# Attention with two gated layers on one core: paired softmax sums, a later second frame, and a regrouped last chunk

## The chip, the cores and the metric

The kernel runs on one core of a Trainium2 chip. The metric is the device time in microseconds of one execution, as the median of several runs. The profile of one execution gives what each engine did and when.

## What is computed

The reference has three parts, on batch 4, sequence 576 and 8 heads of 64. The first is causal attention with a decay that comes from a running sum along the sequence:

```python
cum = np.cumsum(np.maximum(s, 0.0), axis=-1)
scores = scale * q @ k.T + np.minimum(-(cum[..., :, None] - cum[..., None, :]), 0.0)
attn = exp(scores - max);  attn = attn / (attn.sum(-1) + 1e-9);  out = attn @ v
```

The second is a layer of width 1024 with a three-tap convolution and a gate: `h = relu(x @ w_in)`, `(h * sigmoid(conv(h))) @ w_out`. The third mixes along the sequence at rank 32, `u = x + (x.T @ U @ V).T`, and returns `u + relu(u @ w_ch1) @ w_ch2` with 2048 hidden channels.

## The kernel before

All 32 heads run one after the other (`att_head`). A head's scores are made in five blocks of query rows: `scores` takes blocks 0 to 3 of 128 rows, and `scores4` the last 64 rows of two heads at once, in two halves of 288 keys. For each block TensorE multiplies (L690), VectorE adds the mask and finds the row's extreme (L651), ScalarE takes the exponential and the row sum (L668), VectorE adds 1e-9 to the sum and inverts it (L724 and L725 for the four sums of blocks 0 to 3, L763 and L769 for the last block), and GpSimd multiplies the block by the inverse (L679, in `normalise`). TensorE then transposes the block (`transp`, L793) and multiplies it with v (`av`, L829).

Beside this the weights are brought from memory as 64-bit numbers, decoded by ScalarE (L502) and VectorE (L505 once, L515 twice for each piece), and split into a high and a low part (L353 on ScalarE, L365 on GpSimd). The first layer of a batch (`m1_in`, `m1_out`) runs while the attention of the next one does. Then come the sequence mixing (`mix`), the first product of the third part as a seven-product Strassen scheme (`m2_in`, L1178, with sums `S` of weight blocks at L1140 and `T` of activations at L1077), and its second product.

That second product runs in five chunks of tokens, four of 512 and a last one of 256. Of each chunk, `m2_load` brings hidden block f (16 of them), and `m2_out` adds three products for each of four output blocks dt (L1277, 128 rows each) into four accumulators `my`. When f is 15, each accumulator is scaled and added to `u` on VectorE (L1300) and stored (L1308). The hidden blocks sit in a ring of five pairs of tiles, `mh` and `ml`, so block 15 is loaded into the tiles that block 10 leaves.

What sets the order of all of this is a planner. Every step is an entry of a list with an engine, a modelled cost and its dependencies; `Plan.order` simulates the engines with those costs and takes on each engine the ready entry that stands first in the list. The instructions are then issued in that order, and each engine works its own row through in order. So a changed cost, or a dependency that is added, moves instructions of other steps too.

At the start, two tiles `qkFs`, one each for the first two heads, get a frame: VectorE clears 64 rows (L451), and ScalarE's queue brings two rows of ones (L454). The running sum `cum` is brought (L447), clipped (L459) and summed (L460); rows of it go into the tiles (L579 on SP's queue, L582 on ScalarE's). q and k come by L577, v by L591, the mask by L1317, and a unit matrix `ident` by L1323, with two shifted halves of it by L1328.

Transfers of the SP and ScalarE queues share eight completion semaphores (DMAHW0 to DMAHW7), which are handed out in turn. A transfer whose semaphore was used before waits, at the head of its queue, until that earlier transfer has landed.

Of the kernel before, what the change touches and what calls it, by code (L numbers as in the profile page):

```python
# [24 lines left out]
NF1, NF2 = 8, 16  # L25
# [8 lines left out]
NG = 4  # L34
WN = ("A11", "A12", "A22", "S1", "S2", "S3", "S4")
UN = ("B11", "B21", "B22", "T1", "T2", "T3", "T4")

WI, WO, WP, WM = 0.3, 1.5, 0.3, 0.2

# [270 lines left out]
def tile_attention_moe_mixer(  # L310
# [133 lines left out]
    def cum():  # L444
        return cc()

    dma(73728, lambda: nc.sync.dma_start(out=cum(), in_=s), [], [cc])  # L447
    key = [cc]
    for t in qkFs:

        dve(2 * S, lambda t=t: nc.vector.memset(t[0:64], 0.0), [], [(t, "z"), (t, "r0"), (t, "r1")], True)  # L451
        for i in range(2):
            dma_act(
                lambda t=t, i=i: nc.scalar.dma_start(out=t[i : i + 1, i, :], in_=one_d[i, 0:1, 0, :]),  # L454
                [],
                [(t, "z")],
            )

    dve(S, lambda: nc.vector.tensor_scalar(cum(), cum(), 0.0, 8.0, ALU.max, ALU.mult), key, key, True)  # L459
    scan = dve(S, lambda: nc.vector.tensor_tensor_scan(cum(), cum(), cum(), 0.0, ALU.add, ALU.max), key, key)  # L460

    def decay_parts():
        hi_dve(lambda: rk[:, 0, :], cum, key, [(rk, 0)], S)
# [236 lines left out]
    def scores(h, i):  # L700
        P, sm = st[h]["P"][i], st[h]["sm"]
        w = 128 * i + 128
        ps = bank("sc", f"sc{h}_{i}")
        products(h, ps, 128, 128 * i, 0, w)
        top(ps, 128, w, 384 - 128 * i, lambda: sm[:, i : i + 1], None, [], (sm, f"m{i}"))
        exps(
            lambda: P[:, :w],
            ps,
            128,
            w,  # L710
            lambda: sm[:, i : i + 1],
            lambda: sm[:, 4 + i : 5 + i],
            (sm, f"m{i}"),
            [P, (sm, f"s{i}")],
        )
        if i in RECIP:
            ns = range(max((x + 1 for x in RECIP if x < i), default=0), i + 1)
            ss = [(sm, f"s{n}") for n in ns]
            rs = [(sm, f"r{n}") for n in ns]

            def r():
                return sm[:, 8 + ns[0] : 9 + i]

            dve(2, lambda: nc.vector.tensor_scalar(r(), sm[:, 4 + ns[0] : 5 + i], 1e-9, None, ALU.add), ss, rs)  # L724
            dve(15, lambda: nc.vector.reciprocal(r(), r()), rs, rs)  # L725
            for n in ns:
                Pn = st[h]["P"][n]
                normalise(Pn, 128 * n + 128, lambda n=n: sm[:, 8 + n : 9 + n], (sm, f"r{n}"), [Pn])

    def scores4(h):  # L730

        P, sm = st[h]["P"][4], sm4s[h // 2 % 2]
        tiles = []
        for n in range(2):
            ps = bank("sc", f"sc{h}_4_{n}")

            products(h + 1, ps, 128, S - 128, n * HS, HS)
            products(h, ps, 64, S - 64, n * HS, HS)
            top(
                ps,  # L740
                128,
                HS,
                512 * n,
                lambda n=n: sm[:, n : n + 1],
                None if n == 0 else lambda: sm[:, 0:1],
                [] if n == 0 else [(sm, "m0")],
                (sm, f"m{n}"),
            )
            tiles.append(ps)
        for n, ps in enumerate(tiles):  # L750
            exps(
                lambda n=n: P[:, n * HS : n * HS + HS],
                ps,
                128,
                HS,
                lambda: sm[:, 1:2],
                lambda n=n: sm[:, 2 + n : 3 + n],
                (sm, "m1"),
                [(P, n), (sm, f"s{n}")],
            )  # L760
        dve(
            60,
            lambda: nc.vector.scalar_tensor_tensor(  # L763
                sm[:, 4:5], sm[:, 2:3], 1e-9, sm[:, 3:4], ALU.add, ALU.add
            ),
            [(sm, "s0"), (sm, "s1")],
            [(sm, "r")],
        )
        dve(15, lambda: nc.vector.reciprocal(sm[:, 4:5], sm[:, 4:5]), [(sm, "r")], [(sm, "r")])  # L769
        normalise(P, S, lambda: sm[:, 4:5], (sm, "r"), [(P, 0), (P, 1)])  # L770


# [490 lines left out]
        )  # L1263
        hid[c, f] = (mh, ml)

    def m2_out(c, f):
        n, t0 = CHUNKS[c], offs[c]
        mh, ml = hid.pop((c, f))
        if f == 0:
            ys[c] = [bank("my", f"my{c}_{dt}") for dt in range(KT)]  # L1270
        for dt in range(KT):

            def mms(dt=dt):
                c0 = dt * 128
                wh, wl = w2h[f][:, c0 : c0 + 128], w2l[f][:, c0 : c0 + 128]
                for k, (ww, xx) in enumerate(((wh, mh), (wh, ml), (wl, mh))):
                    nc.tensor.matmul(  # L1277
                        ys[c][dt][:, :n], lhsT=ww, rhs=xx[:, :n], start=f + k == 0, stop=f == NF2 - 1 and k == 2
                    )

            pe(3 * mm(n), mms, [w2h[f], w2l[f], mh, ml], [ys[c][dt]])
        if f == NF2 - 1:
            for dt in range(KT):
                o = ring(m2, "o", RINGS["o"], [128, 512], F32, f"o{c}_{dt}")
                t = t0
                while t < t0 + n:
                    b = t // S
                    e = min(t0 + n, (b + 1) * S)
                    dma(
                        (e - t) * 512,  # L1290
                        lambda o=o, t=t, e=e, b=b, dt=dt: nc.sync.dma_start(
                            out=o[:, t - t0 : e - t0], in_=u_t[b][:, dt, t - b * S : e - b * S]
                        ),
                        [(u_d[b], dt)],
                        [(o, t)],
                    )
                    t = e
                dve(
                    n,
                    lambda o=o, dt=dt: nc.vector.scalar_tensor_tensor(  # L1300
                        o[:, :n], ys[c][dt][:, :n], 2.0**-16, o[:, :n], ALU.mult, ALU.add
                    ),
                    [ys[c][dt], o],
                    [o],
                )
                dma(
                    n * 512,
                    lambda o=o, dt=dt: nc.sync.dma_start(out=outT[dt, :, t0 : t0 + n], in_=o[:, :n]),  # L1308
                    [o],
                    [],  # L1310
                )


    prep4(0)
# [10 lines left out]
    for a in (0, 64):  # L1325
# [2 lines left out]
            lambda a=a: nc.sync.dma_start(out=ident[:, 128 + a : 192 + a], in_=ident_d[:, 64 - a : 128 - a]),  # L1328
            [],
            [(ident, 1 + a)],  # L1330
        )

    w1_jobs = [(f, c) for c in (0, 512) for f in range(NF1)]

# [167 lines left out]
    for g in range(2):  # L1502
        blk = (w2a, u1p)[g].buf(f"u{g}", [128, 2 * 7 * S], F32R, f"w2_{g}")
        for i in range(7):
            f = 7 * g + i
            w2h[f] = Part(blk, lambda t, i=i: t[:, 1024 * i : 1024 * i + 512], f"w2h_{f}")
            w2l[f] = Part(blk, lambda t, i=i: t[:, 1024 * i + 512 : 1024 * i + 1024], f"w2l_{f}")

    def load_w2b(f):
        load_split(w2[f], w2h[f], w2l[f], 512, 512, f"w2b_{f}")  # L1510
# [16 lines left out]
    for n in range(len(seq) + LAG):  # L1527
# [3 lines left out]
                n2 += 1  # L1531
            m2_load(*seq[n])
        if n >= LAG:
            m2_out(*seq[n - LAG])
    for p in (m2, mx, u1p, w2a, dec, banks):
        end = p.close()
        end.preds.update(o for o in plan.ops[:-1] if o.eng == "-")
# [57 lines left out]
```

## Time and profile before

| | |
|---|---|
| median of 3 runs | 851.01 us (849.09 to 852.35) |
| the profiled execution | 849.4 us, of which 847.6 us from the first instruction to the last |
| TensorE busy | 813.4 us, 96% of the span |
| VectorE, ScalarE, GpSimd busy | 606.6, 471.0, 392.7 us |
| granted TensorE clock | 0.999 of full speed |

A busy TensorE is not a TensorE at its peak, since matmuls are pipelined and their ends are modelled. Idle time of an engine other than TensorE costs nothing by itself. The span of 847.6 us is 1.8 us shorter than the execution's own time of 849.4 us.

### The profile page before, as it was taken

The numbers are of one execution on the slowest core, as the hardware profiler recorded it, in microseconds if no ns is written. First come the engines' busy times: TensorE is split into PE (matmuls) and PEld (weight loads), VectorE is DVE, ScalarE is ACT, GpSimd is POOL, SyncE is SP. The second block draws the span as 40 slices with busy tenths as digits, with TensorE's granted clock in tenths as the row PEclk, the third lists the DMA queues.
The fourth block names the chain that finished last, engine by engine and source line by source line (L and its number), as shares of the span: only waits on it lengthen the run. The fifth ranks groups of instructions, "written<-read, shape, count | busy, mean of one in ns | idle before, by whom it ended". The sixth has DMA issues, their size and how long they took to land. (4 is left out here: it accounts for less than half of the span.)

```text
span 847.6 us, 15619 instructions
## 1 busy us (share of the span) xinstructions
PE 813.4 (96%) x5300; PEld 736.0 (87%) x5300; DVE 606.6 (72%) x1326; ACT 471.0 (56%) x1176; POOL 392.7 (46%) x489
## 2 busy tenths in 40 slices
PE   5989999999999999999997999999999999999998
PEld 3555899999899999999997999999998888888888
DVE  6876999867997589967799989877588732323232
ACT  4887898867877588767675343433344422222211
POOL 3766875864456536447276667555465200000000
PEclk9999999999999999999999999999999999999999
DMA  6666753662455434402134444645368663545443
GB/s 181 185 169 181 197 118 107 161 163 59 129 145 129 115 82 127 129 25 84 56 106 136 156 145 135 205 155 168 128 215 261 194 185 111 176 118 164 127 124 100
DMA packets 66311, 119.71 MB, mean 141 GB/s; under 512 B 9396, under 2 KB 34868, under 8 KB 66232
## 3 DMA queue, kind: packets, MB, share of 16 engines
q1 hardware_dynamic: 66160, 118.70, 48.7%
q8 instruction: 42, 0.69, 0.3%
q14 instruction: 37, 0.30, 0.1%
q10 hardware_dynamic: 72, 0.01, 0.0%
HBM read 68.81 MB, written 28.90 MB: 115 GB/s over the span
## 5 line engine op out<-in xcount | busy, mean ns | idle before, releaser
L1277 PE MATMUL my<-mh,w 128*128 128x512 f32 (+1 forms) x560 | 158.8, 368 | 0.0
L1258 DVE SCALAR_TENSOR_TENSOR ml<-ml,mh 128x512 fp32r<-128x512 f32 (+1 forms) x80 | 53.2, 673 | 104.4 <-ACT mh L1255 104.4
L1178 PE MATMUL ma_S<-u,W 128*128 128x288 f32 x768 | 119.7, 296 | 5.0 <-DVE s L1194 4.9
L935 PE MATMUL y<-gh,w1o 128*128 128x288 f32 x512 | 118.0, 301 | 0.5 <-DVE c L914 0.5
L1255 ACT ACTIVATE mh<-ml 128x512 fp32r<-128x512 f32 (+1 forms) x80 | 46.9, 589 | 127.7 <-DMA ml<-ch_d 68.8
L1277 PEld LDWEIGHTS my<-mh,w 128*128 128x128 f32 x560 | 101.6, 189 | 17.5
L1178 PEld LDWEIGHTS ma_S<-u,W 128*128 128x128 f32 x768 | 107.5, 188 | 7.4 <-DVE s L1194 7.3
L679 POOL TENSOR_SCALAR P<-P,sm 128x128 f32<-128x128 f32 (+3 forms) x128 | 73.4, 592 | 82.6 <-DVE sm L725 76.6
L1277 PE MATMUL my<-ml,w 128*128 128x512 f32 (+1 forms) x280 | 103.0, 368 | 0.0
L1178 PE MATMUL ma_A<-u,W 128*128 128x288 f32 x576 | 92.8, 296 | 1.6 <-ACT p L1190 1.5
L935 PEld LDWEIGHTS y<-gh,w1o 128*128 128x128 f32 x512 | 86.3, 188 | 1.7 <-DVE c L914 1.1
L1178 PEld LDWEIGHTS ma_A<-u,W 128*128 128x128 f32 x576 | 81.9, 188 | 2.7 <-ACT p L1190 2.2
L365 POOL TENSOR_TENSOR gl<-c,gh 128x288 fp32r<-128x288 f32 x64 | 55.5, 870 | 61.8 <-ACT gh L920 58.5
L651 DVE CUSTOM_DVE_ANT_0 sc<-sc,mask 128x128 f32<-128x128 f32 (+2 forms) x144 | 68.6, 495 | 20.7 <-PE sc L690 19.3
L893 PE MATMUL h<-xh,w1h 128*128 128x290 f32 x256 | 80.0, 312 | 1.1 <-DVE c L914 0.7
L893 PE MATMUL h<-xl,w1h 128*128 128x290 f32 x256 | 76.2, 298 | 0.0
L893 PE MATMUL h<-xh,w1l 128*128 128x290 f32 x256 | 76.1, 297 | 0.0
L935 PE MATMUL y<-gl,w1o 128*128 128x288 f32 x256 | 75.0, 293 | 0.0
L668 ACT ACTIVATE P<-sc,sm 128x128 f32<-128x128 f32 (+3 forms) x128 | 67.6, 531 | 11.5 <-DVE sm L651 9.9
L905 DVE SCALAR_TENSOR_TENSOR c<-h,cw,c 128x288 f32<-128x288 f32 x128 | 64.1, 509 | 5.8 <-ACT c L901 4.9
L362 DVE TENSOR_TENSOR tl<-pt,th 128x384 fp32r<-128x384 f32 x96 | 54.5, 567 | 10.8 <-ACT th L353 10.6
L1277 PEld LDWEIGHTS my<-ml,w 128*128 128x128 f32 x280 | 52.8, 189 | 8.7
(147 smaller groups left out, 1989.6 us busy)
## 6 DMA issues: line engine op xcount, KB each, us to landing
ml<-ch_d SPq DMA_DIRECT2D x64, 256.0 KB
ch_d<-p SPq DMA_DIRECT2D x64, 144.0 KB
raw_w<-w_in SPq DMA_DIRECT2D x16, 512.0 KB
raw_w2a<-w_in SPq DMA_DIRECT2D x16, 512.0 KB
raw_w2b<-w_in SPq DMA_DIRECT2D x16, 512.0 KB
t<-qk_in SPq DMA_DIRECT2D x24, 288.0 KB
qkB<-t SPq DMA_DIRECT2D x24, 288.0 KB
qkA<-t SPq DMA_DIRECT2D x24, 288.0 KB
```

Source lines behind the costliest of these rows:

```text
L362: dve(n, lambda: nc.vector.tensor_tensor(out(), src(), f32(hi()), ALU.subtract), r, w)
L365: pool(n, lambda: nc.gpsimd.tensor_tensor(out(), src(), f32(hi()), ALU.subtract), r, w, two=True)
L651: lambda: nc.vector.tensor_tensor_reduce(out=ps[:rows, :w], in0=ps[:rows, :w], in1=mask[:rows, m0 : m0 + w], scale=-0.125, scalar=3.0e38 i ...
L668: lambda: nc.scalar.activation(out(), ps[:rows, :w], ACTF.Exp, bias=low(), scale=-1.0, accum_out=total()),
L679: lambda: nc.gpsimd.tensor_scalar(t[:, :w], t[:, :w], r(), 1.0, ALU.mult, ALU.mult),
L893: nc.tensor.matmul(ps[:, :W], lhsT=ww, rhs=xx, start=kt + n == 0, stop=kt == KT - 1 and n == 2)
L905: lambda k=k: nc.vector.scalar_tensor_tensor(c(), hh[:, k : k + HS], cw[:, 3 * f + k : 3 * f + k + 1], c(), ALU.mult, ALU.add),
L935: nc.tensor.matmul(ps[:, :HS], lhsT=ww, rhs=xx(), start=f + n == 0, stop=f == NF1 - 1 and n == 2)
L1178: nc.tensor.matmul(ps[:, :HS], lhsT=ww, rhs=uu, start=k == 0, stop=k == 5)
L1255: act(n, lambda: nc.scalar.activation(mh[:, :n], raw(), ACTF.Relu), [ml], [mh])
L1258: lambda: nc.vector.scalar_tensor_tensor(ml[:, :n], raw(), 0.0, f32(mh[:, :n]), ALU.max, ALU.subtract),
L1277: nc.tensor.matmul(ys[c][dt][:, :n], lhsT=ww, rhs=xx[:, :n], start=f + k == 0, stop=f == NF2 - 1 and k == 2)
```

## The change

It has three parts. The sum with 1e-9 and its reciprocal become one entry of the planner's list, `invert`, with a modelled length of 140 elements; before they were two entries, of 2 and 15 elements (blocks 0 to 3) and of 60 and 15 (the last block). In the first part of the kernel the second head's frame is put behind the running sum, and the two shifted halves of `ident` behind the first head's row of `cum`. And in the last chunk, hidden blocks 11 to 15 are no longer taken for all four output blocks before the next hidden block; the list has, for each output block in turn, its products with hidden blocks 11 to 15, then its scaling and its store.

```diff
+END = 5
...
-    for t in qkFs:
+    def frame(t):
...
+    frame(qkFs[0])
+
     dve(S, lambda: nc.vector.tensor_scalar(cum(), cum(), 0.0, 8.0, ALU.max, ALU.mult), key, key, True)
     scan = dve(S, lambda: nc.vector.tensor_tensor_scan(cum(), cum(), cum(), 0.0, ALU.add, ALU.max), key, key)
+    place1 = len(plan.ops)
+    frame(qkFs[1])
+    for o in plan.ops[place1:]:
+        o.preds.add(scan)
...
-            dve(2, lambda: nc.vector.tensor_scalar(r(), sm[:, 4 + ns[0] : 5 + i], 1e-9, None, ALU.add), ss, rs)
-            dve(15, lambda: nc.vector.reciprocal(r(), r()), rs, rs)
+            def invert():
+                nc.vector.tensor_scalar(r(), sm[:, 4 + ns[0] : 5 + i], 1e-9, None, ALU.add)
+                nc.vector.reciprocal(r(), r())
+
+            dve(140, invert, ss, rs)
...
-        dve(15, lambda: nc.vector.reciprocal(sm[:, 4:5], sm[:, 4:5]), [(sm, "r")], [(sm, "r")])
+        def invert():
+            nc.vector.scalar_tensor_tensor(sm[:, 4:5], sm[:, 2:3], 1e-9, sm[:, 3:4], ALU.add, ALU.add)
+            nc.vector.reciprocal(sm[:, 4:5], sm[:, 4:5])
+
+        dve(140, invert, [(sm, "s0"), (sm, "s1")], [(sm, "r")])
...
             lambda a=a: nc.sync.dma_start(out=ident[:, 128 + a : 192 + a], in_=ident_d[:, 64 - a : 128 - a]),
             [],
             [(ident, 1 + a)],
-        )
+        ).preds.add(st["first"])
...
-            m2_out(*seq[n - LAG])
+            c, f = seq[n - LAG]
+            if c < last or f < NF2 - END:
+                m2_out(c, f)
+            if f == NF2 - 1:
+                for dt in range(KT):
+                    m2_rest(c, dt)
+                for dt in range(KT):
+                    if c == last:
+
+                        for f in range(NF2 - END, NF2):
+                            m2_out(c, f, [dt])
+                    m2_end(c, dt)
```

`m2_rest` is the load of `u` and `m2_end` the scaling and the store that stood in `m2_out` before. The planner moves much else with it: on TensorE some 790 of 4012 rows of the first 450 us and of the last chunk stand elsewhere, on VectorE some 440 of 1300.

**SP's queue at the start.** The rows show what each transfer waits for. `qkF_104` is the first head's tile, `qkF_129` or `qkF_139` the second's; `cc` is the running sum, `ws` the mask, `vr` v. Before:

```order
L591 DMA vr_132<-vP_in 128x640
L1317 DMA ws<-mask_in 128x192
L1323 DMA ident<-ident_in 128x128
L1328 DMA ident<-ident_in 128x64 [waits DMAHW1_49]
L1328 DMA ident<-ident_in 128x64 [waits DMAHW2_49]
L579 DMA qkF_104<-cc 1x16x36 [waits DMAHW4_49,DVE_49]
L577 DMA qkF_129<-qk_in 64x1152 [waits DMAHW6_49]
```

Now:

```order
L599 DMA vr_130<-vP_in 128x640
L1328 DMA ws<-mask_in 128x192
L1334 DMA ident<-ident_in 128x128
L585 DMA qkF_139<-qk_in 64x1152 [waits DMAHW0_49]
L482 DMA r_d<-one_in 64x576 [waits DMAHW3_49]
L587 DMA qkF_104<-cc 1x16x36 [waits DMAHW5_49,DVE_49]
L587 DMA qkF_139<-cc 1x16x36 [waits DMAHW6_49,DVE_49]
```

The first head's row of the running sum had two halves of `ident` ahead of it and shared a semaphore with the load of v; now it has the second head's q and k and a block of ones ahead of it, and shares a semaphore (DMAHW5) with the load of the mask.

**VectorE, the first last-block pair (heads 2 and 3).** `sm_1` holds its sums, `wf_w_3` and `wf_w_4` are pieces of weight being decoded, and ISA rows are the mask step and its result. Before:

```order
L651 ISA sc_4_1_383,sm_1_389<-sc_4_1_383,mask,sm_1_389 128x288
L651 ISA sm_1_389 128x1
L515 SCALAR_TENSOR_TENSOR wf_w_3_0_385<-raw_w_3_0_305,wf_w_3_0_385 128x512
L505 TENSOR_SCALAR wf_w_4_0_405<-raw_w_4_0_334 128x512
L362 TENSOR_TENSOR t_8_361<-t_8_361,t_8_366 128x576
L763 SCALAR_TENSOR_TENSOR sm_1_389<-sm_1_389 128x1
L515 SCALAR_TENSOR_TENSOR wf_w_4_0_405<-raw_w_4_0_334,wf_w_4_0_405 128x512
L769 RECIPROCAL sm_1_389<-sm_1_389 128x1
```

Now:

```order
L513 TENSOR_SCALAR wf_w_4_0_401<-raw_w_4_0_338 128x512
L659 ISA sc_4_1_389,sm_1_392<-sc_4_1_389,mask,sm_1_392 128x288
L659 ISA sm_1_392 128x1
L523 SCALAR_TENSOR_TENSOR wf_w_4_0_401<-raw_w_4_0_338,wf_w_4_0_401 128x512 x2
L774 SCALAR_TENSOR_TENSOR sm_1_392<-sm_1_392 128x1
L775 RECIPROCAL sm_1_392<-sm_1_392 128x1
```

Between the mask step and the reciprocal stand two decode steps and the sum, where three decode steps, a split of q and k (`t_8`) and the sum stood. The decode of `wf_w_3` has moved ahead, its first two steps in front of the sum and the reciprocal of head 2's blocks 0 to 3.

**VectorE, where the mixing meets the Strassen products.** `wf_w2a` is the third weight pair being decoded, `S_2` its sums, `T_1` the sums of activations, `s_0_0` the first result that frees an accumulator. Before:

```order
L1077 TENSOR_TENSOR T_1_6394<-u_6259 128x576
L362 TENSOR_TENSOR u_6259<-T_1_6378,u_6259 128x576
L505 TENSOR_SCALAR wf_w2a_0_6413<-raw_w2a_6184 128x512
L362 TENSOR_TENSOR u_6259<-T_1_6394,u_6259 128x576
L515 SCALAR_TENSOR_TENSOR wf_w2a_0_6413<-raw_w2a_6184,wf_w2a_0_6413 128x512
L505 TENSOR_SCALAR wf_w2a_1_6441<-raw_w2a_6300 128x512
L1077 TENSOR_TENSOR T_1_6447<-u_6259,T_1_6378 128x576
L515 SCALAR_TENSOR_TENSOR wf_w2a_0_6413<-raw_w2a_6184,wf_w2a_0_6413 128x512
L515 SCALAR_TENSOR_TENSOR wf_w2a_1_6441<-raw_w2a_6300,wf_w2a_1_6441 128x512 x2
L1140 TENSOR_TENSOR S_2_6496<-wf_w2a_1_6441 128x256
L1194 TENSOR_TENSOR s_0_0_6504<-ma_0_S_6485,p_0_0_6492 128x288
```

Now:

```order
L1085 TENSOR_TENSOR T_1_6401<-u_6269 128x576
L523 SCALAR_TENSOR_TENSOR wf_w2a_1_6375<-raw_w2a_6252,wf_w2a_1_6375 128x512
L364 TENSOR_TENSOR u_6269<-T_1_6390,u_6269 128x576
L364 TENSOR_TENSOR u_6269<-T_1_6401,u_6269 128x576
L523 SCALAR_TENSOR_TENSOR wf_w2a_1_6375<-raw_w2a_6252,wf_w2a_1_6375 128x512
L1085 TENSOR_TENSOR T_1_6447<-u_6269,T_1_6390 128x576
L1148 TENSOR_TENSOR S_2_6455<-wf_w2a_0_6322,wf_w2a_1_6375 128x256
L1148 TENSOR_TENSOR S_2_6462<-wf_w2a_1_6375 128x256
L1148 TENSOR_TENSOR S_2_6462<-S_2_6462,wf_w2a_0_6322 128x256
L1148 TENSOR_TENSOR S_2_6455<-wf_w2a_0_6322,S_2_6462 128x256
L1202 TENSOR_TENSOR s_0_0_6510<-ma_0_S_6492,p_0_0_6500 128x288
```

The whole decode of the pair, six steps, now stands ahead of the last `T_1`, four of them ahead of the stretch shown; before, three steps stood behind it. All four sums `S_2` stand ahead of `s_0_0`, before only one.

## Rows read from the trace of the kernel before

**Rows 1.** Page, part 1: busy time of each engine, share of the span, instructions.

```profile
PE 813.4 (96%) x5300; PEld 736.0 (87%) x5300; DVE 606.6 (72%) x1326; ACT 471.0 (56%) x1176; POOL 392.7 (46%) x489
```

**Rows 2.** Waits of TensorE: us in total, times, longest us.

```profile
PE sc L690 <- DMA qkF<-cc: 8.3, 1, 8.3
...
PE pt L793 <- ACT P L668: 4.6, 5, 1.4
PE t L971 <- DVE s L1194: 2.6, 1, 2.6
PE tp L952 <- ACT x L941: 2.0, 1, 2.0
PE pt L793 <- POOL p L679: 1.9, 2, 1.6
```

**Rows 3.** Windows: busy us (instructions) of PE, PEld, DVE, ACT, POOL; clock; DMA; GB/s.

```profile
80.00:400.00 320.00, 314.11 (x2315) 299.85 (x2314) 263.52 (x701) 249.50 (x683) 189.37 (x280) 1.00 0.47 121
```

**Rows 4.** Timeline of the start: start us, us, engine, line, work, idle before.

```profile
4.17 1.34 DVE L460 TENSOR_TENSOR_SCAN cc<-cc 32x576 f32<-32x576 f32 x1
...
5.22 0.81 SPq L1328 DMA_DIRECT2D ident<-ident_in  x2
...
6.15 0.60 SPq L579 DMA_DIRECT2D qkF<-cc  x1
6.71 0.31 DVE L359 CAST mask<-ws 128x128 bf16<-128x128 f32 x2
...
8.31 7.70 PE L690 MATMUL sc<-qkF 128*128 128x128 f32 x18 [8.31 <-DMA qkF<-cc]
```

**Rows 5.** Timeline of VectorE, 15 us: a sum and its reciprocal next to each other.

```profile
14.81 0.17 DVE L724 TENSOR_SCALAR sm<-sm 128x4 f32<-128x4 f32 x1
15.01 0.18 DVE L725 RECIPROCAL sm<-sm 128x4 f32<-128x4 f32 x1
```

**Rows 6.** Timeline of TensorE, 38 us: transposes of a softmax block.

```profile
37.76 0.30 PE L793 MATMUL pt<-ident,p 128*128 128x128 f32 x1 [1.40 <-ACT P L668]
```

**Rows 7.** Timeline of VectorE, 28 to 37 us.

```profile
30.43 0.43 DVE L505 TENSOR_SCALAR wf_w<-raw_w 128x512 int32<-128x512 int32 x1 [1.56 <-ACT tf L353]
...
32.31 0.71 DVE L515 SCALAR_TENSOR_TENSOR wf_w<-raw_w,wf_w 128x512 int32<-128x512 int32 x1
...
34.41 1.23 DVE L763 SCALAR_TENSOR_TENSOR sm<-sm 128x1 f32<-128x1 f32 x1
...
36.17 0.15 DVE L769 RECIPROCAL sm<-sm 128x1 f32<-128x1 f32 x1
```

**Rows 8.** Timeline of VectorE, 437 to 456 us.

```profile
437.65 1.36 DVE L1077 TENSOR_TENSOR T<-u 128x576 f32<-128x576 f32 x1 [0.90 <-DMA u<-u_d]
...
448.33 0.74 DVE L1077 TENSOR_TENSOR T<-u,T 128x576 f32<-128x576 f32 x1
449.00 4.32 DVE L515 SCALAR_TENSOR_TENSOR wf_w2a<-raw_w2a,wf_w2a 128x512 int32<-128x512 int32 x3
...
454.65 0.45 DVE L1194 TENSOR_TENSOR s<-ma_S,p 128x288 f32<-128x288 f32 x1
455.02 0.57 DVE L1140 TENSOR_TENSOR S<-S,wf_w2a 128x256 f32<-128x256 f32 x1
```

**Rows 9.** Timeline of VectorE, the last chunk: block 15's low part, the last two scalings.

```profile
839.37 0.43 DVE L1258 SCALAR_TENSOR_TENSOR ml<-ml,mh 128x256 fp32r<-128x256 f32 x1 [0.97 <-ACT mh L1255]
...
843.75 0.78 DVE L1300 SCALAR_TENSOR_TENSOR o<-my,o 128x256 f32<-128x256 f32 x2
```

**Rows 10.** Timeline of TensorE, the last chunk: where each three products of one output block begin.

```profile
836.59 0.40 PE L1277 MATMUL my<-mh,w 128*128 128x256 f32 x2
...
836.95 0.40 PE L1277 MATMUL my<-mh,w 128*128 128x256 f32 x2
```

**Rows 11.** Timeline of SP's queue, the last chunk: the last of its four stores.

```profile
844.89 0.40 SPq L1308 DMA_DIRECT2D outT<-o  x1
```

**Rows 12.** Timeline of GpSimd, 34 us: a split of weights.

```profile
34.14 1.48 POOL L365 TENSOR_TENSOR w1l<-wf_w,w1h 128x512 fp32r<-128x512 f32 x1 [0.59 <-ACT w1h L353]
```

More of the change, by code (lines that the diff above doesn't have):

```diff
@@ L760, in scores4 @@
             )
[L761 to L767, printed above, removed]
-        )
-        dve(15, lambda: nc.vector.reciprocal(sm[:, 4:5], sm[:, 4:5]), [(sm, "r")], [(sm, "r")])
+        def invert():
+            nc.vector.scalar_tensor_tensor(sm[:, 4:5], sm[:, 2:3], 1e-9, sm[:, 3:4], ALU.add, ALU.add)
+            nc.vector.reciprocal(sm[:, 4:5], sm[:, 4:5])
+        dve(140, invert, [(sm, "s0"), (sm, "s1")], [(sm, "r")])
         normalise(P, S, lambda: sm[:, 4:5], (sm, "r"), [(P, 0), (P, 1)])
@@ L1264, in m2_load, with m2_out @@
         hid[c, f] = (mh, ml)
-    def m2_out(c, f):
+    def m2_out(c, f, dts=range(KT)):
         n, t0 = CHUNKS[c], offs[c]
-        mh, ml = hid.pop((c, f))
-        if f == 0:
+        mh, ml = hid[c, f]
+        if c not in ys:
             ys[c] = [bank("my", f"my{c}_{dt}") for dt in range(KT)]
-        for dt in range(KT):
+        for dt in dts:
             def mms(dt=dt):
@@ L1281, in m2_out, with m2_rest, m2_end @@
             pe(3 * mm(n), mms, [w2h[f], w2l[f], mh, ml], [ys[c][dt]])
[L1282 to L1311, printed above, removed]
+    outs = {}
+    def m2_rest(c, dt):
+        n, t0 = CHUNKS[c], offs[c]
+        o = outs[c, dt] = ring(m2, "o", RINGS["o"], [128, 512], F32, f"o{c}_{dt}")
+        t = t0
+        while t < t0 + n:
+            b = t // S
+            e = min(t0 + n, (b + 1) * S)
+            dma(
+                (e - t) * 512,
+                lambda t=t, e=e, b=b: nc.sync.dma_start(
+                    out=o[:, t - t0 : e - t0], in_=u_t[b][:, dt, t - b * S : e - b * S]
+                ),
+                [(u_d[b], dt)],
+                [(o, t)],
+            )
+            t = e
+    def m2_end(c, dt):
+        n, t0 = CHUNKS[c], offs[c]
+        o = outs[c, dt]
+        dve(
+            n,
+            lambda: nc.vector.scalar_tensor_tensor(
+                o[:, :n], ys[c][dt][:, :n], 2.0**-16, o[:, :n], ALU.mult, ALU.add
+            ),
+            [ys[c][dt], o],
+            [o],
+        )
+        dma(n * 512, lambda: nc.sync.dma_start(out=outT[dt, :, t0 : t0 + n], in_=o[:, :n]), [o], [])
     prep4(0)
@@ L1330, in tile_attention_moe_mixer @@
             [(ident, 1 + a)],
-        )
+        ).preds.add(st["first"])
     w1_jobs = [(f, c) for c in (0, 512) for f in range(NF1)]
@@ L1507, in tile_attention_moe_mixer @@
             w2l[f] = Part(blk, lambda t, i=i: t[:, 1024 * i + 512 : 1024 * i + 1024], f"w2l_{f}")
+    last = len(CHUNKS) - 1
     def load_w2b(f):
```

## The prediction

> **What bounds the kernel.** I read the page's busy times first: TensorE is busy for 96% of the span, VectorE for 72% [rows 1]. So a change pays only where TensorE stands idle, some 34 us in all, or after its last matmul. TensorE's list of waits says where: 8.3 us before the first matmul, 4.6 and 1.9 us in front of transposes of softmax blocks, 2.6 and 2.0 us where the mixing meets the Strassen products [rows 2]. In the bulk of the attention (80 to 400 us) TensorE idles only 6 us of 320 and VectorE 56 [rows 3], so a little more work on VectorE is hidden there. The timelines of the start, of the first heads, of that meeting point and of the last chunk give the terms below.
>
> **How the times stand to each other.** The sum is made against the profiled execution, 849.4 us, 1.6 us below the median of 851.0; I put the difference on the median. 0.5%, about what a measurement of this kernel can tell from no change, is 4.3 us.
>
> **The change, part by part.**
>
> *Start.* TensorE begins at 8.31, released by a row of the running sum [rows 4]. That row was issued by SP at 6.15: the running sum ended at 4.17 + 1.34 = 5.51, but SP was busy with the halves of `ident` until 5.22 + 0.81 = 6.03, and had to wait for v, whose semaphore it reuses. So the second frame, which the change takes away in front of the running sum, was not the last thing waited for. In the changed kernel the sum ends earlier, at most by the time that one frame takes on VectorE, and ScalarE's row with it. But SP's row now waits for the mask, which is queued behind v, and ahead of it stand the second head's q and k and a block of ones. Lower bound: the mask lands when the first q and k do, 5.22 [rows 4]; the row goes 0.9 us earlier. Upper bound: the mask has landed by 6.71, when VectorE reads it; the row goes 0.6 later. I take 0.1 later, near the row that exists, since v, just ahead of the mask, is what held it: +0.1 us (−0.9 to +0.6). The second head's rows come later too, but its scores are the fifth product in TensorE's row, behind the four of the first head, which covers them. The halves of `ident` are first used by transposes later still. The first weight piece is queued behind two more transfers, some 0.8 us of SP's issuing (two halves of `ident` took 0.81, [rows 4]); VectorE's decode of it now stands behind two more mask steps, which cover it. If they did not, that 0.8 us would show.
>
> *Sum and reciprocal as one entry.* There are 48 pairs; in 19 the two already stood next to each other, in 29 one to three other steps stood between. Now all are adjacent. An adjacent pair takes 0.20 us from start to start where others overlap [rows 5], so VectorE pays at most 0.1 us more for each of 29, 2.9 us in all, against 56 us of idle time [rows 3]: nothing. What it buys is that the multiplication by the inverse, and so the transposes, start earlier by the steps that stood between. Of TensorE's idle time, 1.9 us waits for that multiplication, 1.6 of it in one place [rows 2]. There one short mask step stood between. I take −0.3 us (0 to −0.6).
>
> *The order that the planner makes of it, early.* The largest wait for a softmax block, 1.40 us, is at 37.76 [rows 6]. It is behind the reciprocal that ends at 36.17 + 0.15 = 36.32. From its mask step, done when the decode step of 32.31 begins [rows 7], to that end VectorE ran three decode steps, a split and the sum, 4.0 us. Now two decode steps of 0.7 us [rows 7], the sum and the reciprocal stand there, some 1.8 us, since the decode of `wf_w_3` has moved ahead, to where VectorE was idle for 1.56 us in front of a decode step [rows 7]. So the reciprocal comes up to 2 us earlier, and the wait of 1.40 can go. Bounds 0 and −1.4; I take −1.0, because the sum may again last 1.23 us. Of the other waits for softmax blocks (3.2 us) the order rows give no sign; I take 0 and keep them for the rivals.
>
> *Where the mixing meets the Strassen products.* TensorE waits 2.0 us for ScalarE's copy of `x`, which is queued behind a cast of the last `T_1`, and 2.6 us for `s_0_0` [rows 2]. VectorE is the cause: it stood idle for 0.90 at 437.65 and then ran without a pause, three decode steps of 1.44 us each among it, until `s_0_0` at 454.65 [rows 8]. Now the decode starts ahead of that idle time (−0.9). Three more sums `S_2` of about 0.57 stand ahead of `s_0_0` (+1.7). The three decode steps moved to a place where GpSimd splits less; they last between 0.7 [rows 7] and 1.44 us, so 0 to −2.2 us, and I take −1.0. Together −0.2 us (−1.9 to +1.7). The first wait grows, since three decode steps are added ahead of the last `T_1`, and the second shrinks by the same.
>
> *Last chunk.* Block 15 is now wanted earlier. Its load still waits for block 10's end, about 836.7; its low part was ready at 839.37 + 0.43 = 839.8 [rows 9]. The planner has put twelve groups of other blocks and one of accumulator 3 in front of it, thirteen of 0.36 us [rows 10], so it is wanted at about 841.4. No wait: 1.6 us to spare. At the end, accumulators 0 to 2 finish four groups before the last one, so their stores are out of SP's way. Before, the last store was issued at 844.89, though its data were ready at 843.75 + 0.78 = 844.53 [rows 9, 11]: −0.35 us (0 to −0.6, if the four stores also slowed each other).
>
> Sum: +0.1 − 0.3 − 1.0 − 0.2 − 0.35 = −1.75 us. Forecast 851.0 − 1.75 = **849.3 us**, or 847.7 for an execution like the profiled one. Its own range is 847.0 to 851.5.
>
> **Rivals.**
>
> *More of the waits go.* The attention's waits for softmax blocks come to 4.6 + 1.9 = 6.5 us [rows 2], of which I count 1.3. If the longer modelled pair orders VectorE better everywhere, two thirds of the rest, 3.4 us, go as well: 845.9 us. For it: what holds these transposes is always this chain. Against: the waits are spread over many places with different causes. Chance 0.22.
>
> *The sum is held up wherever it stands.* The sum at L763 took 1.23 us in [rows 7], and ended at 35.64, when GpSimd's split ended, 34.14 + 1.48 = 35.62 [rows 12]; the row before the change thus shows the wait, not the work. If the pair meets such a split in its new place, the 1.0 and 0.3 us are not gained: 850.6 us. By the Trainium skill's page "SBUF — State Buffer", section "Who interferes with whom" and the lines on its diagram, VectorE with two inputs in SBUF and a GpSimd instruction that reads SBUF lock each other out for a whole instruction, and whoever comes first wins. The trace agrees, to 0.02 us; by that rule alone the two terms would be nothing and the sum −0.45 us. Chance 0.17.
>
> *Decode steps in front of the softmax: slower.* VectorE works its row in order. In the new order decode steps stand ahead of sums and mask steps that they followed before; the first two of `wf_w_3` ahead of head 2's own sum. A decode step that waits for its weight now holds back the softmax. In the row that exists one waited 1.56 us [rows 7]. It decides from the point where a weight lands later than the exponentials are done. Sixteen pieces are decoded in the first hundred microseconds; if three of them wait for 1.3 us each in front of a sum, TensorE loses 3.9 us: 853.2 us, slower than before. Against it: loads are issued well ahead. Chance 0.18.
>
> **How the numbers follow.** The forecast keeps 0.43. The range, 845.0 to 854.0, takes in the four cases; beyond it stay about 0.1 on each side. Faster by over 0.5% (below 846.8) needs the first rival, or nearly all lower bounds at once: 0.22. Slower by over 0.5% (above 855.3) needs the last rival at its worst: 0.08. Within 0.5%: 0.70.
>
> **What would show it right or wrong.** In the profile of the changed kernel: the first matmul starts between 7.4 and 8.9, and not a full microsecond earlier; the 1.40 us in front of the third group of transposes is gone or below 0.5; the two waits at 450 to 456 us become one, of 4 to 5 us together; TensorE has no gap in the last 10 us, and the last store is issued within 0.1 us of its scaling's end. Wrong would be: TensorE's idle time between 20 and 450 us changed by over 3 us either way, a new wait of VectorE in front of a decode step, or a gap before block 15.

## The result, and the profile after

The changed kernel takes 856.88 us (856.25 to 857.02), beside 850.23 (849.09 to 852.35) for the kernel before on the same chip, four runs each: a ratio of 1.0085, 95% interval 1.0067 to 1.0102. It is slower by 6.7 us, where 849.3 us was forecast and 854.0 was the upper end. The profiled execution took 857.02, its span is 855.2; before they were 849.4 and 847.6, so the two traces stand 7.6 us apart.

The page's first part and its line of clocks, after:

```profile
PE 817.6 (96%) x5300; PEld 738.1 (86%) x5300; DVE 612.4 (72%) x1326; ACT 471.5 (55%) x1176; POOL 391.4 (46%) x489
...
PEclk9999999999999999999998999999999999999999
```

The instructions are the same in number as in [rows 1]; VectorE is busy for 5.8 us more. TensorE's list of waits, after (us in total, times, longest us):

```profile
PE sc L698 <- DMA qkF<-cc: 8.8, 1, 8.8
PE pt L801 <- ACT P L676: 5.7, 6, 1.4
PE ma_A L1186 <- DVE s L1202: 2.6, 1, 2.6
...
PE h L901 <- DVE c L922: 2.2, 2, 1.8
PE tp L960 <- ACT x L949: 2.1, 1, 2.1
...
PE pt L801 <- POOL p L687: 0.6, 2, 0.3
```

Beside [rows 2], ScalarE's softmax blocks (`P`) are waited for 1.1 us longer, the last blocks (`p`) 1.3 us less, and both waits at the mixing are still there. What grew most are the waits for VectorE's convolution (`c`). Before, below the rows of [rows 2], there are three:

```profile
PE h L893 <- DVE c L914: 0.7, 1, 0.7
PE y L935 <- DVE c L914: 0.5, 2, 0.2
PE tp L952 <- DVE c L914: 0.4, 1, 0.4
```

That is 1.6 us in all; after, with the 1.1, 0.8 and 0.4 of three further rows, it is 4.5. To see where the 7.6 us came, TensorE's instructions are paired. Its timeline after, at some of those that also stand in the kernel before:

```profile
39.26 0.30 PE L801 MATMUL pt<-ident,p 128*128 128x128 f32 x1 [1.40 <-ACT P L676]
...
122.25 0.40 PE L901 MATMUL h<-xh,w1h 128*128 128x290 f32 x1 [1.78 <-DVE c L922]
...
457.47 1.09 PE L960 MATMUL tp<-ident,x 128*128 128x128 f32 x8 [2.12 <-ACT x L949]
...
461.14 1.81 PE L1186 MATMUL ma_A<-u,W 128*128 128x288 f32 x6 [2.58 <-DVE s L1202]
...
502.62 1.06 PE L1186 MATMUL ma_A<-u,W 128*128 128x288 f32 x6 [1.12 <-ACT p L1198]
```

The start of the same instruction in the two traces:

| TensorE's instruction | before | after | later by |
|---|---|---|---|
| first product | 8.31 | 8.76 | 0.45 |
| transposes that waited 1.40 | 37.76 | 39.26 | 1.50 |
| transposes that waited 0.83 (0.84 before) | 69.51 | 70.38 | 0.87 |
| transposes that waited 0.99 in both | 229.66 | 234.18 | 4.52 |
| transposes of `x` | 450.75 | 457.47 | 6.72 |
| a later Strassen product, which waits for ScalarE's copy `p` | 493.74 | 502.62 | 8.88 |
| end of the span | 847.6 | 855.2 | 7.6 |

So 0.9 us are lost up to 70, 3.6 between 70 and 230, 2.2 from there to 450, 2.2 where the mixing meets the Strassen products, and 1.3 are won back later, 0.4 of them in the last chunk.

### The profile page after: what moved, and what is told of

Its sections match the earlier page's. It is cut to its first block, busy times and chain, and to the rows that moved or that the text cites. A ratio compares the mean times of both kernels' runs of the same rounds, so it can differ in the third digit from the quotient of the medians.

```text
span 855.2 us, 15618 instructions
## 1 busy us (share of the span) xinstructions
PE 817.6 (96%) x5300; PEld 738.1 (86%) x5300; DVE 612.4 (72%) x1326; ACT 471.5 (55%) x1176; POOL 391.4 (46%) x489
```

## The experiments

**Which of the three parts it is.** Four kernels: the change's two `invert` entries alone, its frame and `ident` parts alone, its last chunk alone (no more than the hunks shown with the change), and the change without the two `invert` entries.

> The kernel before with one edit of the three: sum and reciprocal one entry of modelled size 140. The planner then moves 248 of VectorE's 1328 rows. Theory 'order' (the time went because the list's new order puts decode steps and recombination sums in front of what TensorE waits for): most of the +6.7 us, 853 to 857 us. Theory 'adjacency' (holding the two steps together itself delays VectorE): 855 to 857 us. Theory 'start' (the frame and the halves of the identity cost it): 850 us, within 0.7 of before.

> The kernel before with the second frame behind the running sum and the identity halves behind the first scores, nothing else. It moves 152 of VectorE's rows too. Theory 'order': 849 to 853 us, either side of before by up to 3, with a start later by 0.3 to 0.6 us. Theory 'adjacency': 850.2 us plus the 0.45 us of the start. Theory 'start': 855 us or more.

> The kernel before with the last chunk's end one block of rows at a time, nothing else; only 21 of TensorE's rows move, all in the last 20 us. All theories: 849.8 us (-0.45, as the shift of the end against the last 150 us showed in the changed kernel; bounds 0 and -0.8). If it is not below before by 0.2 to 0.8, the gain at the tail was something else.

> The changed kernel without the pair: second frame and identity halves later, and the last chunk's end by blocks. If the parts add up (e2 +0.3, e3 -0.3): 849.6 us, 849.0 to 850.4. If the loss of 6.6 us needs the parts together: above 852.

| kernel | median us | before | ratio |
|---|---|---|---|
| pair alone | 857.6 | 849.61 | 1.0091 (1.0075 to 1.0107) |
| frame alone | 850.23 | 849.61 | 1.0003 (0.9993 to 1.0013) |
| last chunk alone | 849.29 | 849.61 | 0.9992 (0.9980 to 1.0005) |
| all but the pair | 849.45 | 849.66 | 0.9996 (0.9987 to 1.0006) |

The pair has the whole loss; the other two parts are too small to measure, together too. The −0.45 that was expected of the last chunk is within what the times cannot tell; in the traces, TensorE's lag behind the kernel before shrinks by 0.41 us in the last chunk of each kernel that has this part.

**Is it the pair itself, or the order that the planner makes of it?** First the old order, with nothing but each reciprocal moved up to its sum:

```diff
+row = self.order()
+for first, second in self.pairs:
+    row.remove(second)
+    row.insert(row.index(first) + 1, second)
```

> The kernel before with its own order, in which each reciprocal is pulled up to stand right behind its sum; 29 of VectorE's rows move, by one to three places, and no other engine's. Theory 'order': 849.5 to 850.8 us, no difference to be measured. Theory 'adjacency': 854 to 857 us, as after. The prediction's term for adjacency alone: -0.3 us.

852.02 against 849.61 for the kernel before: 1.0028 (1.0018 to 1.0038), 1.5 to 3.2 us lost. VectorE in the kernel before, where a step stood between:

```profile
110.46 0.16 DVE L724 TENSOR_SCALAR sm<-sm 128x4 f32<-128x4 f32 x1
110.53 0.55 DVE L362 TENSOR_TENSOR tl<-pt,th 128x384 fp32r<-128x384 f32 x1
111.00 0.17 DVE L725 RECIPROCAL sm<-sm 128x4 f32<-128x4 f32 x1
111.08 0.49 DVE L651 CUSTOM_DVE_ANT_0 sc<-sc,mask,sm 128x288 f32<-128x288 f32 x1
```

And the same three steps in this experiment:

```profile
111.97 0.16 DVE L729 TENSOR_SCALAR sm<-sm 128x4 f32<-128x4 f32 x1
112.16 0.18 DVE L730 RECIPROCAL sm<-sm 128x4 f32<-128x4 f32 x1
112.25 0.53 DVE L367 TENSOR_TENSOR tl<-pt,th 128x384 fp32r<-128x384 f32 x1
```

Apart, sum and reciprocal delay the step behind them by 0.07 and 0.08 us; next to each other by 0.19 and 0.09. That is 0.13 us more at this place; if it holds for all 29 pairs (the median over them in the two traces is 0.12), it is 3.8 us of VectorE's row, and by the medians 2.4 of it come through.

Is VectorE's row as tight as that? In the old order each of the 48 sums is written twice, 48 small steps more:

```diff
+for _ in range(2):
     nc.vector.tensor_scalar(r(), sm[:, 4 + ns[0] : 5 + i], 1e-9, None, ALU.add)
```

> The kernel before, its order unchanged on every engine, in which each of the 48 sums in front of a reciprocal is issued twice in a row: some 0.07 to 0.17 us of VectorE each, 3.4 to 8 us in all. Theory 'small steps show' (the 2.4 us of e4 were 29 steps of up to 0.1 us that were not hidden, because the softmax chain of the first heads and VectorE's row stand on TensorE's path): +2 to +6 us, 851.6 to 856. Rival 'hidden', as the prediction had it: within 0.7 us of before, 849.0 to 850.4.

857.5 against 849.66: 1.0089 (1.0077 to 1.0101). The page's first part there:

```profile
PE 816.5 (95%) x5300; PEld 737.2 (86%) x5300; DVE 617.6 (72%) x1374; ACT 472.0 (55%) x1176; POOL 392.5 (46%) x489
```

VectorE is busy for 11.0 us more (617.6 against 606.6), and the kernel is 7.8 us slower: VectorE's small steps are not hidden. The traces of these two kernels say where. At the transposes of 70, of 230 and of `x`, TensorE is 1.2, 0.5 and 1.5 us behind the kernel before with the pairs adjacent, and 1.5, 3.8 and 6.8 us behind with the sums twice.

Then the change with only the modelled length altered, in both `invert` entries alike, so that every instruction is the same and only the planner's list differs:

```diff
-dve(140, invert, ss, rs)
+dve(80, invert, ss, rs)
```

> The changed kernel with one number changed: the pair's modelled size is 80 instead of 140 (153 instead of 216 ns in the planner's list). The pairs stay adjacent, the instructions are the same; 109 of VectorE's 1328 rows stand elsewhere. Theory 'order': the time moves by more than 1 us, 849 to 855.5 (or above 858). Theory 'adjacency': no difference from after, 856.2 to 857.6.

> The changed kernel with the pair's modelled size 110 instead of 140 (185 instead of 216 ns in the list), nothing else. Theory 'order': any value between 850 and 858 us, and among the sizes 80, 110, 140 and 170 a spread of 3 us or more that does not follow the size. Rival 'the size is the lever' (smaller is faster): between 854.0 and 856.9, and e12 above 857. Theory 'adjacency': 856.2 to 857.6.

> The changed kernel with the pair's modelled size 170 instead of 140 (247 instead of 216 ns), nothing else. Theory 'order': any value between 850 and 858 us. Rival 'the size is the lever': above 857. Theory 'adjacency': 856.2 to 857.6.

| modelled length | 80 | 110 | 140 (the change) | 170 |
|---|---|---|---|---|
| median us | 854.04 | 855.23 | 856.88 | 853.02 |
| ratio to before | 1.0051 | 1.0058 | 1.0085 | 1.0034 |

The four lie 3.9 us apart and do not follow the length. The size of this spread is rough, since a second set of runs of the change, below, has a median 3.2 us higher; but no execution with 80, 110 or 170 (850.9 to 856.1) is as long as the change's shortest, 856.25. All are slower than before, and by these ratios by as much as the adjacency alone or more: the pairs cost about 2.4 us, and the order that comes out adds from 0.5 (less than the intervals can tell from nothing) to 4.8. Sum and order are taken to add up here, which no run shows by itself.

**Is VectorE's load what holds the early part?** The change and the kernel before, both with VectorE relieved in the first 120 us: the third decode step of the 16 pieces of `w1` runs on 2 of 512 columns.

```diff
+*((oi()[:, :2], half(i, I32)[:, :2], sc, oi()[:, :2]) if i and few else (oi(), half(i, I32), sc, oi())),
```

> The changed kernel, which leaves out part of the computation: the third decode step of each of the 16 weight pieces of w1 handles 2 columns instead of 512, so some 13 us of VectorE's work are gone between 10 and 160 us and the order of every engine stays. Theory 'VectorE is full there' (between 80 and 212 us VectorE, 91 per cent busy, sets the pace, and any less lucky order costs): TensorE gains 4 to 7 us by 212 us, 850 to 853 in all. Rival 'other engines' (GpSimd, ScalarE or TensorE's own order make the loss of 3.6 us in that stage): under 2 us gained, 855 to 857.

> The kernel before with the same part left out as in e6: 2 columns instead of 512 in the third decode step of the 16 pieces of w1. Theory 'VectorE is full there': it gains 1.5 to 3.5 us (its gaps of TensorE in that stage), 846.5 to 848.5, and the distance between the two kernels falls from 6.6 to 7.3 us to about 3.5, the part that came behind 212 us. Rival 'other engines': the distance stays above 6.

The change then takes 851.27 (1.0022, 1.0010 to 1.0033), the kernel before 845.73 (0.9944, 0.9929 to 0.9958). The relief is worth 5.6 us in the one and 3.9 in the other: in the kernel before, too, TensorE waits early on for VectorE's row. Their distance is 5.5 us, not the 3.5 that was expected; at the transposes of 230 us it is 2.2 in the traces, instead of 4.5. So in these traces half of what the change loses up to there hangs on VectorE's load; by the medians the whole distance shrinks less, from 6.7 to 5.5.

**One place in the attention.** The longest new wait of TensorE is the 1.78 at 122.25. VectorE of the changed kernel ahead of it:

```profile
117.71 1.60 DVE L523 SCALAR_TENSOR_TENSOR wf_w<-raw_w,wf_w 128x512 int32<-128x512 int32 x1
119.24 0.93 DVE L913 SCALAR_TENSOR_TENSOR c<-h,cw,c 128x288 f32<-128x288 f32 x2
120.09 1.32 DVE L513 TENSOR_SCALAR wf_mix<-raw_mix 128x160 int32<-128x160 int32 x1
121.33 0.51 DVE L913 SCALAR_TENSOR_TENSOR c<-h,cw,c 128x288 f32<-128x288 f32 x1
121.76 0.44 DVE L922 SCALAR_TENSOR_TENSOR c<-c,h 128x288 f32<-128x288 f32 x1
```

ScalarE there:

```profile
119.35 0.62 ACT L355 CAST w1o<-wf_w 128x512 fp32r<-128x512 f32 x1 [0.81 <-DVE wf_w L523]
119.87 0.44 ACT L919 ACTIVATE c<-c 128x288 f32<-128x288 f32 x1
```

Two decode steps, of 1.60 and 1.32 us, stand within the convolution of two blocks, where they stood behind it in the old order. ScalarE idles 0.81 for the first and then runs its cast ahead of the convolution's activation. That ends at 119.87 + 0.44 = 120.31, but VectorE's L922, which frees the bank of `h`, stands behind the second decode step and starts at 121.76; TensorE waits for it. The experiment moves the two decode steps behind that convolution again (five and six rows down on VectorE), with the cast (five on ScalarE) and the split (one on GpSimd) that follow them:

```diff
+for o, down in zip(self.moved, (5, 6, 5, 1)):
+    line = lines[o.eng]
+    n = line.index(o)
+    line.remove(o)
+    line.insert(n + down, o)
```

> The changed kernel with one piece of work of w1 and one of the mixing weights put behind the convolution at 117 to 122 us, all else in its order: on VectorE the last decode step of w1's last piece goes behind the gate product of block 6, the first decode step of the mixing weights behind that of block 7; ScalarE's cast of that piece goes five places down, GpSimd's low part one. Theory 'decode in front of the convolution' (the 1.78 us wait at 122.25 is one of the places where the new order loses): that wait is gone or below 0.3 us, and TensorE is 1.0 to 1.8 us earlier at 212 us than in the changed kernel's profile; the time falls by as much, to 855.1 to 855.9. Rival 'taken back' (VectorE is full there, the steps are owed a few us later): the wait shows again in front of other products before 165 us, and TensorE at 212 us is within 0.5 us of the changed kernel.

> The changed kernel itself, as the base for e15 on the same chip: 856.9 us, 856.2 to 857.6, and its lag behind the kernel before at 212 us again 4.5, give or take 0.5.

855.73 against 850.32: 1.0066 (1.0054 to 1.0077). The wait of 1.78 is gone, and the transposes of 234.18 start 1.5 us earlier than in the change's trace. The change itself, again on that chip, gave 860.04 (1.0115, 1.0094 to 1.0136), above what was expected: three of its six executions took 857.3 to 858.7 and three 861.4 to 862.0. Against its first median the move wins 1.2 us, but the two intervals overlap; the gain is shown by the traces and not by the times. Nor is this place the cause of the whole: with the pair alone TensorE has no such wait, and the same transposes start at 234.27, as late as in the change.

**Are the small steps worth taking away?** The sum adds 1e-9 to a number that is 1 or more; these two kernels take the reciprocal of the sums directly in the 32 cases where that can be done (blocks 0 to 3), once with the old order and the last chunk's part, once with the change.

```diff
-nc.vector.tensor_scalar(r(), sm[:, 4 + ns[0] : 5 + i], 1e-9, None, ALU.add)
-nc.vector.reciprocal(r(), r())
+nc.vector.reciprocal(r(), sm[:, 4 + ns[0] : 5 + i])
```

> The kernel of e3 (before, with the last chunk's end by blocks) in its own order, without the 32 sums of four columns: the reciprocal reads the row sums themselves. What is left out is the addition of 1e-9 to sums that hold the exponential of 0, so are 1 or more; float32 does not keep it. Theory 'small steps show' (e9: 48 more sums cost 7.8 us, 0.16 each): the 32 are worth 32 x 0.07 to 0.16, -2 to -5 us, 844.5 to 847.5, below both kernels. Rival 'one-sided' (more small steps cost, but fewer gain nothing since other waits stand right behind): 848.8 to 849.8.

> The changed kernel in its own order, without the same 32 sums (so of these pairs only the reciprocal is left; the 16 pairs of the fifth blocks stay). Theory 'small steps show': adjacency's dependent pair goes as well, -3 to -6 us, 851 to 854, and what is left above before is the order's share, 1 to 4 us. Rival 'one-sided': 856 to 857.

With the old order 849.03 (0.9997, 0.9985 to 1.0008), no gain. In the change 855.04 (1.0061, 1.0049 to 1.0074), 1.8 us less than its median, and between the two expectations. More small steps cost in the old order; fewer do not pay there. No kernel that computes the whole beat the kernel before by more than the measurement's uncertainty.

**The mixing.** Three rows were pulled forward, `x` and the first `p1` by two on ScalarE, the first `s` by four on VectorE, to see if the two waits there go:

```diff
+for o, up in zip((x, *self.firsts), (2, 2, 4)):
+    line = lines[o.eng]
+    n = line.index(o)
+    line.remove(o)
+    line.insert(n - up, o)
```

> The changed kernel with three instructions moved at the handover to the Strassen products, all else in its order: on ScalarE the last copy of x and the first copy of p go two places up, ahead of the cast of the last T and the cast of W that they stood behind; on VectorE the first s goes four places up, ahead of the sums S. Theory 'in-order rows at the handover' (the waits of 2.1 and 2.6 us and the clock that drops behind them cost what came between 440 and 470 us): the two waits shrink below 1 us together, the granted clock stays at 1.00, and the time falls by 4 to 7 us to 850 to 853. Rival 'weights' (the products wait for the parts of W and would wait anyway): the waits reappear in front of later products, 856 to 857 us.

857.7 against 849.65: 1.0098 (1.0081 to 1.0115), no gain over the change. TensorE there:

```profile
465.33 0.69 PE L999 MATMUL t<-xth,uhl 128*64 128x512 f32 x1 [4.44 <-ACT xth L373]
```

And ScalarE:

```profile
464.18 0.62 ACT L373 CAST W<-S 128x512 fp32r<-128x512 f32 x1 [3.22 <-DVE S L1168]
464.70 1.07 ACT L373 CAST xth<-tp 128x512 fp32r<-128x512 f32 x2
```

The two waits became one of 4.44 us. The cast of `xth` that TensorE wants is queued behind a cast of weights, for which ScalarE idled 3.22 us, waiting for VectorE's sum `S`. VectorE works without a pause from 449 to 465 us in this trace, 5.3 us of it on the four sums `S`. So it is VectorE's row, with the decoded weights and their sums, that is late here, not the three rows.

## Why the prediction was wrong

**Start: inside its bounds.** TensorE began at 8.76, 0.45 later; −0.9 to +0.6 was given, 0.1 taken. SP issued the row at 6.32, 0.17 later; the rest came between its issue and the first product.

**Sum and reciprocal as one entry: this step failed.** It said that at most 0.1 us for each of 29 was paid "against 56 us of idle time: nothing", and then −0.3. The size was nearly right, 0.13 in the rows above; the cover was not there. The adjacency in the old order cost 2.4 us, and 48 more steps 7.8, with the 56 us of idle time in place. That idle time is an average over stages. The windows of the kernel before:

```profile
80.00:165.00 85.00, 83.71 (x604) 77.94 (x603) 77.22 (x217) 73.56 (x211) 60.58 (x88) 1.00 0.57 148
165.00:400.00 235.00, 230.40 (x1714) 221.90 (x1713) 186.31 (x486) 175.94 (x473) 128.78 (x193) 1.00 0.44 112
```

From 80 to 165 VectorE is busy for 77.22 of 85 us, 91%; behind 165 for 79%. But the price was not paid in the fuller stage alone. In the one trace of each, with the pairs adjacent in the old order TensorE's lag falls from 1.2 to 0.5 us between 70 and 230 and grows by 1.0 from there to the transposes of `x`; with the sums twice it grows by 2.3 and by 3.0. So an engine that idles for a fifth of its time still does not hide these steps. By [rows 5] the price could be read; that idle time covers it was taken without a row that shows it. What the pair was to buy did come, and more: the waits for GpSimd's multiplication fell from 1.9 to 0.6 us. But those for ScalarE's exponentials (`P`) grew by 1.1, so it did not become time.

**The early order: this step failed.** It took the sum with its two decode steps for 1.8 us and the wait of 1.40 for gone. VectorE after:

```profile
34.01 2.39 DVE L523 SCALAR_TENSOR_TENSOR wf_w<-raw_w,wf_w 128x512 int32<-128x512 int32 x2
36.32 0.62 DVE L774 SCALAR_TENSOR_TENSOR sm<-sm 128x1 f32<-128x1 f32 x1
36.97 0.16 DVE L775 RECIPROCAL sm<-sm 128x1 f32<-128x1 f32 x1
```

GpSimd after:

```profile
34.75 2.18 POOL L358 TENSOR_SCALAR t<-t 128x576 fp32r<-128x576 f32 x2
```

The two decode steps took 2.39 us, not 1.4, and the sum ended at 36.32 + 0.62 = 36.94, when GpSimd's pair of splits did, 34.75 + 2.18 = 36.93. The wait is again 1.40, and its transposes start 1.5 us later than before. At this place the second rival, that the sum is held up wherever it stands, was right: the same meeting as in [rows 7, 12], with another split. But the reciprocal starts only 0.80 later (36.97 against 36.17). The rest comes behind it, and the reading of [rows 6] left it out: what ended the wait is ScalarE's exponential of a later block, which needs a mask step behind the reciprocal on VectorE. GpSimd's multiplication by the inverse had ended earlier, at 36.42 + 0.75 = 37.17 before and 37.31 + 1.12 = 38.43 after. Before and after, on ScalarE:

```profile
37.05 0.47 ACT L668 ACTIVATE P<-sc,sm 128x256 f32<-128x256 f32 x1
```

```profile
38.55 0.47 ACT L676 ACTIVATE P<-sc,sm 128x256 f32<-128x256 f32 x1
```

It too is 1.5 us later, since in the new order a split of q and k (`t`) stands on VectorE between the reciprocal and that mask step:

```profile
37.05 0.76 DVE L364 TENSOR_TENSOR t<-t,t 128x576 fp32r<-128x576 f32 x1
```

**The mixing: this step failed.** −0.2 was forecast, with two waits that become one of 4 to 5. Both are there still, 2.12 and 2.58 [rows 2]. TensorE lost 2.2 us here. One term was far off: the three more sums `S` were put at about 0.57 us each, and lasted 1.4 to 1.6:

```profile
456.14 1.62 DVE L1148 TENSOR_TENSOR S<-wf_w2a 128x256 f32<-128x256 f32 x1
457.80 1.51 DVE L1148 TENSOR_TENSOR S<-S,wf_w2a 128x256 f32<-128x256 f32 x1
459.34 1.38 DVE L1148 TENSOR_TENSOR S<-wf_w2a,S 128x256 f32<-128x256 f32 x1
```

The other terms made up for it: `s` starts 5.50 us after the last `T` does (460.64 and 455.14), where it was 6.32 [rows 8]. What no term had is TensorE's clock. Between the two waits the old order has eight transposes and six Strassen products (`ma_A`), the new one the transposes alone. Windows of the kernel before, and then of the kernel with the last chunk alone, which has the old order here:

```profile
448.00:468.00 20.00, 15.38 (x111) 14.06 (x110) 18.17 (x30) 12.93 (x26) 11.27 (x9) 1.00 0.53 166
```

```profile
448.00:468.00 20.00, 15.40 (x101) 13.84 (x100) 17.02 (x26) 12.65 (x25) 11.23 (x9) 0.91 0.43 143
```

And of the changed kernel, 7 us later and in parts:

```profile
455.00:475.00 20.00, 15.30 (x92) 13.78 (x91) 14.06 (x22) 12.46 (x25) 10.24 (x9) 0.83 0.34 114
...
455.00:460.00 5.00, 1.44 (x11) 0.96 (x9) 4.93 (x6) 2.76 (x7) 4.04 (x3) 0.97 0.97 320
460.00:465.00 5.00, 3.86 (x16) 3.65 (x17) 2.28 (x4) 2.58 (x6) 4.08 (x5) 0.50 0.05 20
```

The clock granted falls from full speed to half, 1.2 GHz, within the second wait (0.97 in the window that ends at 460, 0.50 in the next). From the first wait's end to the later product that waits for `p` the kernel before takes 42.99 us at full clock; the seven other traces with the old order here, all with a fall, take 44.46 to 44.60; the changed kernel takes 45.15. So about 1.5 of the 2.2 us goes with the fall of the clock, which the old order pays as well in these seven traces; that the trace of before has none is luck, and part of the 7.6 us between the two traces. The other 0.7 is open, and not in every trace of the new order: with the pair alone it takes 44.22. With the modelled length 110, whose second wait lies behind the six products as in the old order, the clock stayed up and it takes 42.95.

**Last chunk: right.** −0.35 was forecast, −0.41 came in the trace. No gap before block 15, and the store goes out as its scaling ends, 852.14 + 0.42 = 852.56:

```profile
852.14 0.42 DVE L1316 SCALAR_TENSOR_TENSOR o<-my,o 128x256 f32<-128x256 f32 x1 [1.01 <-PE my L1285]
...
852.60 0.33 SPq L1322 DMA_DIRECT2D outT<-o  x1
```

**What the sum left out.** It priced four places and gave the other rows of the list nothing, though the order rows showed some 440 of 1300 moved on VectorE. Between 70 and 450 us the changed kernel loses 5.8 us, and for that stretch the sum had only the −0.3 of the pairs. Of this, the convolution place is shown (its removal gave back 1.5 us in the trace), and TensorE's waits for the convolution together grew by 2.9 us; the adjacency runs through all of it; how the rest divides among places stays open. The third rival, decode steps in front of the work that TensorE wants, had the nearest time, 853.2, but another mechanism: in it the decode waits for its weight. Here the weights were there (VectorE's waits in front of the decode of `w1` fell from 5.8 to 4.5 us, none of them for a weight); decode steps were themselves stretched and, at the place shown, stood in front of the convolution, not of the softmax. That its number came nearest is luck. The chance of 0.08 for a loss over 0.5% rested on it alone.

Open is also why 32 fewer steps gain nothing in the old order: in that kernel's trace TensorE was 2.6 us ahead by 400 us and gave 1.6 back at the mixing, with the clock at half for a stretch; whether the medians hide the same was not tried.

## What to carry to other kernels

An engine's idle share does not show that its small steps are hidden: 48 more of them cost 7.8 us with VectorE 72% busy, and in the trace 3.0 of that were lost between 230 and 450 us, where it idled for a fifth. Put the step in twice and measure before calling a cost covered. An edit to an entry of a list that a planner sorts is an edit to the whole order; the choice of one modelled length among four moved this kernel by 3.9 us, so bound it by the list's own scatter, not by the two or three places that look better. In this kernel two small steps that need each other were better left with another step between them.

## What was not expected of the hardware

A decode step without a second input lasted over several GpSimd instructions. In the run with three rows pulled forward, VectorE:

```profile
103.51 3.09 DVE L531 TENSOR_SCALAR wf_w<-raw_w 128x512 int32<-128x512 int32 x1
```

and GpSimd, which ran without a pause meanwhile:

```profile
102.99 1.32 POOL L385 TENSOR_TENSOR w1o<-wf_w,w1o 128x512 fp32r<-128x512 f32 x1
104.26 0.48 POOL L376 TENSOR_SCALAR vv<-vr 128x320 fp32r<-128x320 f32 x1
104.68 0.81 POOL L385 TENSOR_TENSOR gl<-c,gh 128x288 fp32r<-128x288 f32 x1
105.44 0.88 POOL L385 TENSOR_TENSOR vv<-vr,vv 128x320 fp32r<-128x320 f32 x1
```

The step ended at 106.60, GpSimd's fourth instruction at 106.32; the same form took 0.43 in [rows 7], and the same step 1.10 in the changed kernel's trace:

```profile
102.70 1.10 DVE L513 TENSOR_SCALAR wf_w<-raw_w 128x512 int32<-128x512 int32 x1
```

There GpSimd ran the same first instruction, and the step ended behind that one (103.80 and 103.52). The run with the modelled length 110 shows 3.08 us, again over all four. The execution with the 3.09 took 860.5 us beside a median of 857.7; beside the changed kernel's trace, 3.3 us are lost near 104 us. The same cause would fit the two groups of times of the changed kernel's second run, but none of its three longer executions has a trace, so that is only argued. In the changed kernel the smaller step of `wf_mix` at 120.09, which took 0.23 us in the kernel before, also ended (121.41) just behind GpSimd's split:

```profile
120.04 1.27 POOL L367 TENSOR_TENSOR w1o<-wf_w,w1o 128x512 fp32r<-128x512 f32 x1
```

which ends at 121.31. By the Trainium skill's page "SBUF — State Buffer", section "Who interferes with whom", a `tensor_scalar` too can, if its operands allow it, take the port pair that VectorE shares with GpSimd, and then whoever comes second waits for the other's whole instruction; the 1.32 us for 160 columns agree with it. That one VectorE instruction waits for four of GpSimd's, as in the 3.09 us, goes beyond that sentence, and what decides it is open.
